# Slots of 256 rows run between the units of attention, with two experts' weights fetched ahead

## The chip, the cores and the metric

The kernel runs on one core of one Trainium2 chip. The metric is the device time of one execution in microseconds; beside it stands one profiled execution, whose trace gives every row shown here. TensorE is called PE (its weight loads PEld), VectorE DVE, ScalarE ACT, GpSimd POOL and SyncE SP.

## What is computed

Block-sorted attention feeds a layer of eight experts, of which each row uses one.

```python
# attention: B, H, S, D = 4, 8, 768, 64; 8 blocks of 96 rows
P = sort_net;  5 times: P = softmax over the last axis, then divided by its sum over the axis before
k_sorted, v_sorted = P applied to the blocks of k and v
attn = softmax(q_block @ k_sorted_block.T / sqrt(D));  x = attn @ v_sorted_block   # x: 3072 x 512
# experts: E, F = 8, 1024
logits = x @ w_gate + modality_bias[modality_id]
e_idx = argmax(logits);  gate_w = softmax(logits)[e_idx]
out[rows of e] = gate_w * (relu(x @ w1[e]) @ w2[e])
```

The inputs drawn for the reference send 1513 of the 3072 rows to expert 0 and 1559 to expert 3; no other expert gets one.

## The kernel before

The order of all instructions on each engine is that of the code (a manual schedule). Three parts follow each other.

Preparation and sort: POOL issues the loads of k, v and q of the first two batches (g = 0). DVE runs the five Sinkhorn steps and puts pieces of `spread_k` between them, which copy k into a zero-padded layout; POOL copies the other half. `make_bd` builds block-diagonal matrices, and the sort multiplies k and v with them, 8 matmuls (k) or 4 (v) into one PSUM bank, with two such banks; each bank is evacuated by `sort_k` or `sort_v` on DVE or ACT.

Attention: 32 units of half the blocks of one head for two batches. A unit has `prep_q` (a spread on DVE, six transposes, a copy), `scores`, `expo` on ACT and `av` with its normalization on DVE. The 28 sort jobs of the other two batches (g = 1) are put into units 2 to 15, two a unit. The gate's transposes and matmuls (`gate_T`, `gate_L`) trail by one octet of units. After each octet m, `choose` finds the expert of each of its 768 rows and `place` scatters the rows to a DRAM scratch sorted by expert, with eight indirect DMAs on POOL. `load_w` is called for experts 0 to 3 behind the first scatter, for all eight after attention and for all eight once more; a flag per expert makes each DMA conditional.

Experts: 25 slots of 128 rows after attention (`run`, lines of `mX`, `mL1`, `mH`, `mL2`). A slot loads its rows with SP, transposes them (line 593), multiplies with w1 (line 599, 8 matmuls of 512 columns, the rows being the stationary side), applies relu, transposes the result (line 626), multiplies with w2 (line 599, 8 matmuls of 512) and scatters the scaled rows to the output. Which expert a slot has stands in a table; PE loads the offset into a register (line 607) and adds a constant to it for each matmul. That addition is an instruction of PE's sequencer of its own (FUSED_REGOPS in the trace, ISA in the order). Slots 0 to 10 need only the first three octets; the last octet's scatter, table and padding (`pad_fill`) run between them.

Of the kernel before, what the change touches and what calls it, by code (L numbers as in the profile page):

```python
# [17 lines left out]
def kernel(  # L18
# [21 lines left out]
    NT = N // 128  # L40
# [3 lines left out]
    CAP = N + 128  # L44
    S1, SU, SMAX = 11, 25, 31
    S2 = SMAX - S1
# [3 lines left out]

    xs_dram = nc.dram_tensor("xs_scratch", [E * CAP + 128, GW // 2], I32, kind="Internal").ap()
# [22 lines left out]
    g_off = k_off + 2 * BLK * D
    xTg = [w_all[:, g_off + z * 768:g_off + (z + 1) * 768].rearrange("p (t r) -> p t r", t=8) for z in range(2)]

    v_sb = [singles.tile([128, 128, VW], BF16, tag=f"v_sb{g}", name=f"v_sb{g}") for g in range(2)]
    v_sbf = [t.rearrange("p x d -> p (x d)") for t in v_sb]
    k_raw = v_sbf[1][:, 0:BLK * D]
    attnT = [singles.tile([96, 8 * BLK + 32], BF16, tag=f"attnT{z}", name=f"attnT{z}") for z in range(2)]  # L80
    xb = [singles.tile([BLK, 8, GW], BF16, tag=f"xb{z}", name=f"xb{z}") for z in range(2)]
    ubuf = singles.tile([128, 8 * 768 + 2 * 1536], BF16, tag="ubuf")

    def qT_buf(g, h):
        base = ubuf if g == 0 else w_all
        x0 = h * 768 + (0 if g == 0 else k_off)
        return base[:, x0:x0 + 768]

    def qil_buf(g, hq):
        if g == 0:  # L90
            return v_sbf[1][:, BLK * D:BLK * D + 1536]
        x0 = k_off + 8 * 768 + (hq % 2) * 1536
        return w_all[:, x0:x0 + 1536]

    qin_bufs = [ubuf[:, 8 * 768 + z * 1536:8 * 768 + (z + 1) * 1536] for z in range(2)]

    ident = singles.tile([128, 128], BF16)
    P_t = singles.tile([BH, NB, NB], FP32)
    nc.sync.dma_start(out=P_t, in_=sort_net.rearrange("b h i j -> (b h) i j"))
    k_src = k.rearrange("b h (n c) d -> (b h n) (c d)", n=NB)  # L100
    v_src = v.rearrange("b h (n c) d -> (b h n) (c d)", n=NB)

    def load_k(g):
        for kc in range(KCH):
            cs = slice(kc * KCW * D, (kc + 1) * KCW * D)
            nc.gpsimd.dma_start(out=k_raw[:, cs], in_=k_src[g * 128:(g + 1) * 128, cs])

    def spread_k(kc, par):
        rows = slice(par * 64, (par + 1) * 64)
        cs = slice(kc * KCW * D, (kc + 1) * KCW * D)  # L110
        eng = nc.gpsimd if par else nc.vector
        eng.tensor_copy(k_il[rows, kc * KCW:(kc + 1) * KCW, par],
                        k_raw[rows, cs].rearrange("p (c d) -> p c d", d=D))

    def load_v(g):
        nc.gpsimd.dma_start(out=v_in, in_=v_src[g * 128:(g + 1) * 128])

    def load_q(g, hq):
        t = qin_bufs[hq % 2].rearrange("p (r h f) -> p r h f", r=2, h=2)
        for par in range(2):  # L120
            nc.gpsimd.dma_start(out=t[:, par], in_=q[2 * g + par, 2 * hq:2 * hq + 2]
                                .rearrange("h (p t) d -> p h (t d)", t=6))
# [26 lines left out]
    bias0 = singles.tile([BLK, E], FP32)  # L149
    nc.sync.dma_start(out=bias0, in_=moe_modality_bias[0:1].broadcast_to([BLK, E]))  # L150
    biasd = singles.tile([BLK, E], FP32)
    nc.sync.dma_start(out=biasd, in_=moe_modality_bias[1:2].broadcast_to([BLK, E]))
    wg_sb = singles.tile([128, 4, E], BF16)

# [9 lines left out]
                   ap=[ident.ap[0], [1, NB], [NB, 16]])  # L164
    for it in range(5):
# [4 lines left out]
        if it == 0:  # L170
            nc.vector.tensor_reduce(jmask, id3s, AX.X, ALU.add)
        elif it == 1:
            nc.vector.tensor_reduce(bmask, id3, AX.X, ALU.add)
            for g in range(2):
                nc.vector.tensor_copy(sel[g], ident[0:BH, g * 16:(g + 1) * 16].broadcast_to([BH, 16, NB]))
        else:
            spread_k(it - 2, 0)
# [9 lines left out]
    bd_v, bd_k = [], []  # L187

    def make_bd(g):
# [9 lines left out]
        bv = singles.tile([128, 16, NB], BF16, tag=f"bdv{g}", name=f"bdv{g}")  # L199
        rb = bass.AP(tensor=rr.tensor, offset=rr.offset, ap=[rr.ap[0], [0, 16], rr.ap[1]])  # L200
        nc.vector.tensor_tensor(bv, bmask.broadcast_to([128, 16, NB]), rb, ALU.mult)
        bk = singles.tile([128, 8, NB], BF16, tag=f"bdk{g}", name=f"bdk{g}")
        nc.vector.tensor_tensor(bk, bv[:, 0:8], bv[:, 8:16], ALU.add)
        bd_v.append(bv.rearrange("p a b -> p (a b)"))
        bd_k.append(bk.rearrange("p a b -> p (a b)"))

    make_bd(0)
    v_cols = v_flat.rearrange("p (c d) -> p d c", d=D)

    def sort_k(g, ch, act):  # L210
        acc = mipsum.tile([128, 8, 64], FP32, tag="mi", name=f"ka{g}_{ch}")
        for z in range(8):
            nc.tensor.matmul(acc[:, z], k_il[:, ch * 8 + z].rearrange("p r d -> p (r d)"), bd_k[g],  # L213
                             start=True, stop=True)
        dst = kTb[g].rearrange("p (x c) -> p x c", c=BLK)[:, :, ch * 8:(ch + 1) * 8]
        (nc.scalar.copy if act else nc.vector.tensor_copy)(dst, acc.rearrange("p z x -> p x z"))  # L216

    def sort_v(g, ch, act):
        acc = mipsum.tile([128, 4, 128], FP32, tag="mi", name=f"va{g}_{ch}")
        for z in range(4):  # L220
            nc.tensor.matmul(acc[:, z], v_cols[:, ch * 4 + z], bd_v[g], start=True, stop=True)  # L221
        dst = v_sb[g][0:BLK, :, ch * 4:(ch + 1) * 4]
        (nc.scalar.copy if act else nc.vector.tensor_copy)(dst, acc[0:BLK].rearrange("p z x -> p x z"))  # L223

    sort_jobs = [[(sort_k, g, ch) for ch in range(12)] + [(sort_v, g, ch) for ch in range(16)]
                 for g in range(2)]
    for n, (f, g, ch) in enumerate(sort_jobs[0]):
        f(g, ch, n % 2)
        if n == 11:
            load_k(1)  # L230
            make_bd(1)
    load_v(1)

    from concourse.masks import make_upper_triangular
    maskUT = singles.tile([128, 128], BF16)
    make_upper_triangular(nc, maskUT, val=1.0, diag=False)
    ones_bf = singles.tile([128, 128], BF16)
    nc.gpsimd.memset(ones_bf, 1.0)
    ones8 = singles.tile([128, E], FP32)
    nc.gpsimd.memset(ones8, 1.0)  # L240
    nc.gpsimd.dma_start(out=wg_sb, in_=moe_w_gate.rearrange("(c p) e -> p c e", p=128))
    ebase = singles.tile([BLK, E, E], BF16)
    nc.gpsimd.memset(ebase, 0.0)
    for e in range(1, E):
        nc.gpsimd.memset(ebase[0:1, :, e:e + 1], float(CAP * e))
    tiew = singles.tile([BLK, E], FP32)
    for e in range(E):
        nc.gpsimd.memset(tiew[:, e:e + 1], float(E - e))
    pI = singles.tile([128, 1], I32)
    nc.gpsimd.iota(pI, pattern=[[0, 1]], base=0, channel_multiplier=1)  # L250
    pF = singles.tile([128, 1], FP32)
    nc.gpsimd.tensor_copy(pF, pI)
    sI = singles.tile([128, SMAX], I32)
# [530 lines left out]
```

## Time and profile before

| | us |
|---|---|
| median of 3 runs (lowest to highest) | 308.87 (305.28 to 310.0) |
| the profiled execution | 309.65 |
| its span, first to last instruction | 307.5 |
| busy: PE, DVE, POOL, ACT | 208.3, 150.0, 113.5, 98.3 |

[...] Instructions of a sequencer (register additions, waits, issues) count as no busy time of their engine.

### The profile page before, as it was taken

How to read it: one execution, taken by the hardware profiler on the slowest of the kernel's cores; microseconds unless marked ns; L12 is line 12 of the kernel's file. 1: busy time of each engine (PE TensorE's matmuls, PEld its weight loads, DVE VectorE, ACT ScalarE, POOL GpSimd, SP SyncE). 2: the span in 40 equal slices, each digit the busy share in tenths (PEclk: the TensorE clock that was granted, in tenths of full speed). 3: DMA queues.
4: the chain of work that ended last, by engine and by line, in shares of the span. 5: the costliest groups of instructions: out<-in, count | busy, mean ns of one | idle time of the engine just before them, and what ended most of it. 6: DMA issues, size and time to landing. Idle time of an engine off the chain costs nothing. (4 is left out here: it accounts for less than half of the span.)

```text
span 307.5 us, 5922 instructions
## 1 busy us (share of the span) xinstructions
PE 208.3 (68%) x1929; PEld 140.3 (46%) x1929; DVE 150.0 (49%) x442; ACT 98.3 (32%) x163; POOL 113.5 (37%) x237
## 2 busy tenths in 40 slices
PE   0007634389998850289770699689949999999930
PEld 0006533277886750277550355345524555555510
DVE  7985537956575560276980255543312323333300
ACT  2003421144756510054420033223422344434420
POOL 8970045504038503074471017812041322333330
PEclk9999999995555555555555599979986999999995
DMA  6998239403402799811120302424153232331110
GB/s 100 224 190 161 47 48 202 61 0 49 59 15 77 115 207 209 133 54 54 29 75 21 103 2 88 130 94 137 55 163 95 71 99 86 106 104 70 50 63 2
DMA packets 21072, 28.05 MB, mean 91 GB/s; under 512 B 5935, under 2 KB 16431, under 8 KB 20784
## 3 DMA queue, kind: packets, MB, share of 16 engines
q0 software_dynamic: 12704, 23.11, 34.7%
q1 hardware_dynamic: 8336, 4.52, 6.1%
q8 instruction: 19, 0.31, 0.4%
q14 instruction: 13, 0.11, 0.1%
HBM read 106.11 MB, written 10.91 MB: 381 GB/s over the span
## 5 line engine op out<-in xcount | busy, mean ns | idle before, releaser
L599 PEld LDWEIGHTS <-ubuf 128*128 128x128 bf16 x400 | 39.1, 101 | 43.2 <-issue 7.9
L599 PE MATMUL hp<-w_all,ubuf 128*128 x200 | 50.0, 395 | 3.3 <-issue 2.4
L645 POOL DMA_INDIRECT out_dram<-v_sb,ix x25 | 24.8, 990 | 70.3 <-ACT ubuf L627 42.2
L599 PE MATMUL yp<-w_all,ubuf 128*128 x200 | 49.8, 394 | 0.4 <-DVE ubuf L627 0.4
L414 POOL DMA_INDIRECT xs_scratch<-xb,dest x32 | 30.2, 943 | 41.5 <-issue 20.4
L616 DVE TENSOR_SCALAR ubuf<-hp 128x512 bf16<-128x512 f32 x25 | 17.3, 692 | 46.0 <-PE hp L599 44.8
L618 ACT ACTIVATE ubuf<-hp 128x512 bf16<-128x512 f32 x25 | 14.9, 597 | 66.5 <-DVE ubuf L616 60.5
L314 ACT ACTIVATE attnT<-sc 96x768 bf16<-96x768 f32 x32 | 25.2, 808 | 17.4 <-PE sc L308 17.4
L329 DVE TENSOR_TENSOR xb<-op,rs 96x256 bf16<-96x256 f32 x64 | 26.9, 420 | 2.2
L637 ACT ACTIVATE v_sb<-yp,v_sb 128x512 f32<-128x512 f32 x25 | 17.2, 687 | 22.3 <-PE yp L599 22.3
L627 DVE COPY ubuf<-ht 128x512 bf16<-128x512 bf16 x25 | 10.6, 423 | 25.5 <-PE ht L626 25.4
L325 PE MATMUL op<-v_sb,attnT 96*128 96x65 bf16 x256 | 20.5, 243 | 0.1
L213 PEld LDWEIGHTS <-w_all 128*128 128x128 bf16 x192 | 11.1, 126 | 19.6 <-issue 19.1
L221 PE MATMUL va<-bdv,w_all 128*128 128x128 bf16 x128 | 17.1, 307 | 4.1 <-DVE v_sb L223 2.1
L593 PE MATMUL mx<-ident,v_sb 128*128 128x128 bf16 x100 | 10.6, 234 | 13.7 <-DMA v_sb<-xs_scratch 13.7
L294 PE MATMUL tq<-ident,w_all 128*128 128x128 bf16 x48 | 6.6, 308 | 18.7 <-DVE w_all L128 18.7
L223 ACT CAST v_sb<-va 96x512 bf16<-96x512 f32 x24 | 13.6, 583 | 16.6 <-PE va L221 15.5
L626 PE MATMUL ht<-ident,ubuf 128*128 128x128 bf16 x200 | 16.7, 226 | 2.6 <-DVE ubuf L594 2.4
L626 PEld LDWEIGHTS <-ubuf 128*128 128x128 bf16 x200 | 14.1, 101 | 9.0 <-issue 3.6
L328 DVE RECIPROCAL rs<-op 96x4 f32<-96x4 f32 x64 | 11.0, 172 | 13.9 <-PE op L325 13.7
L216 ACT CAST w_all<-ka 128x512 bf16<-128x512 f32 x18 | 10.2, 586 | 22.9 <-PE ka L213 22.8
L325 PEld LDWEIGHTS <-attnT 96*128 96x128 bf16 x256 | 17.2, 133 | 0.6 <-DVE xb L329 0.6
(170 smaller groups left out, 308.7 us busy)
## 6 DMA issues: line engine op xcount, KB each, us to landing
w_all<-in_moe_w_dram POOLq DMA_DIRECT2D x40, 1024.0 KB
v_sb<-xs_scratch SPq DMA_DIRECT2D x25, 129.0 KB, 2.0
v_sb<-in_k_dram POOLq DMA_DIRECT2D x6, 512.0 KB
w_all<-in_v_dram POOLq DMA_DIRECT2D x2, 1536.0 KB
ubuf<-in_q_dram POOLq DMA_DIRECT2D x16, 192.0 KB
xs_scratch<-v_sb SPq DMA_DIRECT2D x9, 129.0 KB, 2.2
xs_scratch<-xb,dest POOLq DMA_INDIRECT x32
out_dram<-v_sb,ix POOLq DMA_INDIRECT x25
```

Source lines behind the costliest of these rows:

```text
L221: nc.tensor.matmul(acc[:, z], v_cols[:, ch * 4 + z], bd_v[g], start=True, stop=True)
L223: (nc.scalar.copy if act else nc.vector.tensor_copy)(dst, acc[0:BLK].rearrange("p z x -> p x z"))
L314: nc.scalar.activation(attnT[u % 2][:, 0:8 * BLK].rearrange("p (r f) -> p r f", r=2), sc_tiles.pop(u)[0:BLK, :, 0:4 * BLK], ACT.Exp, scale ...
L325: nc.tensor.matmul(op[:, j], attnT[u % 2][:, c0:c0 + 128], v_sb[g][0:BLK, par * 64 + h * 8 + i, 0:D + 1], start=True, stop=True)
L329: nc.vector.tensor_tensor(xt[:, par * 4:(par + 1) * 4, h * D:(h + 1) * D], op[0:BLK, :, 0:D], rs.broadcast_to([BLK, 4, D]), ALU.mult)
L414: ins = nc.gpsimd.indirect_dma_start(out=xs_dram, out_offset=bass.IndirectOffsetOnAxis(ap=dest[:, t:t + 1], axis=0), in_=xt.bitcast(I32)[: ...
L599: ins = nc.tensor.matmul(*a, **kw).ins
L616: nc.vector.tensor_scalar(hd, hp[:, half], 0.0, None, ALU.max)
L618: nc.scalar.activation(hd, hp[:, half], ACT.Relu)
L626: nc.tensor.transpose(tp[:, c], h_b[s % 2][:, fc * 128:(fc + 1) * 128], ident)
L637: nc.scalar.activation(y, yp, ACT.Copy, scale=xt.bitcast(FP32)[:, Dm // 2 + 1:Dm // 2 + 2])
L645: ins = nc.gpsimd.indirect_dma_start(out=out, out_offset=bass.IndirectOffsetOnAxis(ap=ix, axis=0), in_=y, in_offset=None, bounds_check=N - ...
```

## The change

The program is rewritten around five things.

1. Nothing of k is spread any more. `sort_k` multiplies k as it was loaded, once for each of the two batches, into the two halves of the partitions: 16 matmuls of 64 columns where 8 were. PSUM is divided anew: four banks `mi` for everything, one pair `sc`, one pair `op`. The first sort uses all of them.
2. The two experts with the largest biases of the two modalities are taken as "home" experts and renumbered 0 and 1 (`home_map`). Their weights alone get a buffer, `w01`. The first is fetched after the first sort, the second in unit 9 behind the first scatter, with all of q of the other batches behind it.
3. Slots have 256 rows and belong to one octet each: 2, 3, 3 and 5 slots, 13 in all. A table of 18 small operations on DVE is made after each octet.
4. `mL1` multiplies with the weights as the stationary side and the rows as the moving one (256 columns), so that its result is transposed already; `mH` is gone. A slot has 8 transposes, 32 matmuls of 256 columns and 16 of 512.
5. A slot is cut into seven pieces, and the pieces are put between the parts of the units: three a unit in units 14 to 18, two a unit in units 22 to 31, the other 57 after attention. Rows that those slots leave over go through a general loop at the end, which the drawn inputs do not enter: 1513 rows make 6 slots and 1559 make 7.

The core of the diff:

```diff
-    S1, SU, SMAX = 11, 25, 31
+    PR = 256
+    SLOTS = [(0, 2), (2, 3), (5, 3), (8, 5)]
+    NS = 13
...
-    scpsum = ctx.enter_context(tc.psum_pool(name="scpsum", bufs=2))
-    opsum = ctx.enter_context(tc.psum_pool(name="opsum", bufs=2))
-    mipsum = ctx.enter_context(tc.psum_pool(name="mipsum", bufs=2))
+    scpsum = ctx.enter_context(tc.psum_pool(name="scpsum", bufs=1))
+    opsum = ctx.enter_context(tc.psum_pool(name="opsum", bufs=1))
+    mipsum = ctx.enter_context(tc.psum_pool(name="mipsum", bufs=4))
...
+        for z in range(n):
+            for par in range(2):
+                nc.tensor.matmul(acc[par * 64:(par + 1) * 64, z], k_raw[:, (c0 + z) * D:(c0 + z + 1) * D],
+                                 bd[g][:, par * 64:(par + 1) * 64], start=True, stop=True)
...
+    def load_w(z, tab=None, n=None, parts=(0, 1)):
+        tb, n = (etab, z) if tab is None else (tab, n)
+        er = nc.values_load(tb[0:1, n:n + 1], engines=(PoolEng,), min_val=0, max_val=E - 1)
+        v1, v2 = w_views(z)
+        if 0 in parts:
+            nc.gpsimd.dma_start(out=v1, in_=moe_w1[bass.ds(er, 1)].rearrange("o (c p) f -> p (o c) f", p=128))
...
-                w_mm(s, hp[:, half], xT_b[s % 3][:, c],
-                     w_all[:, bass.ds(ev + (c * F + half * 512), 512)], start=(c == 0), stop=(c == 3))
+    def mL1(s, j):
+        ev = evs[s]
+        hp = mipsum.tile([128, 2, PR], FP32, tag="mi", name=f"hp{s}_{j}")
+        for f in range(2):
             for c in range(4):
+                nc.tensor.matmul(hp[:, f], w_at(ev, c * F + (2 * j + f) * 128, 128), xT_b[s % 2][:, c],
+                                 start=(c == 0), stop=(c == 3))
...
+            at2(8 * m + 9, choose, m)
+            at2(8 * m + 9, place, m)
+            at1(8 * m + 10, table_x, m)
+    at2(9, load_w, 1)
+    at2(9, load_q, 1, 0)
+    at2(9, load_q, 1, 1)
...
+    pieces = []
+    for s in range(NS):
+        if s == 0:
+            pieces.append([(mE, (0,)), (mX, (0,))])
+        for j in range(4):
+            pieces.append([(mL1, (s, j))])
+        if s + 1 < NS:
+            pieces.append([(mE, (s + 1,)), (mX, (s + 1,))])
+        pieces.append([(mL2, (s, 0))])
+        pieces.append([(mL2, (s, 1))])
...
+        if u < 14:
+            return 0, 0
+        if u < 19:
+            return 2, 1
+        if u < 22:
+            return 0, 0
+        return 1, 1
...
+        p1, p2 = pace(u)
+        scores(u)
         expo(u)
+        for f, a in A1.get(u, []):
+            f(*a)
+        run_pieces(p1)
+        if u >= 1:
+            av(u - 1)
         prep_q(u + 2)
+        for f, a in A2.get(u, []):
+            f(*a)
+        run_pieces(p2)
```

How the rows stand on the engines shows in three places. On PE, the first matmuls of a slot before, where `ubuf` is the transposed rows and `w_all` the weights:

```order
L607 TENSOR_LOAD tab_462
L607 ISA x2
L599 LDWEIGHTS ubuf
L599 ISA
L599 MATMUL hp_2397<-w_all,ubuf 128x512
L599 LDWEIGHTS ubuf
L599 ISA
L599 MATMUL hp_2397<-w_all,ubuf 128x512
```

and of the change, where `w_72` is the buffer `w01` and `qT_76` holds the transposed rows:

```order
L572 ISA
L572 LDWEIGHTS w_72
L572 ISA
L572 MATMUL hp_0_1547<-qT_76,w_72 128x256
L572 ISA
L572 LDWEIGHTS w_72
L572 ISA
L572 MATMUL hp_0_1547<-qT_76,w_72 128x256
```

The register addition stood once per matmul of 512 columns; it stands twice per matmul of 256, since the weight load now has the address that is known only at run time. On POOL, in unit 9 of the change, the last of eight scatters (line 439), then the second weight (lines 529 to 534) and q (line 116):

```order
L439 DMA xs_scratch<-xb_85,dest_1206 26880x258
L529 TENSOR_LOAD etab
L529 ISA x2
L532 ISA
L532 DMA w_72<-in_moe_w_dram 128x4x1024
L534 ISA
L534 DMA w_72<-in_moe_w_dram 128x8x512
L116 DMA q_in_80<-in_q_dram 128x4x384 x4
```

Before, q of the same batches stood behind four conditional weights, of which two moved bytes; now it stands behind one. On PE at the start of unit 18 of the change, the last scores (line 340), the count for the table (line 460), and the transposes of the rows of slot 2 (line 553):

```order
L340 MATMUL sc_1887<-qT_77,kT_75 128x96
L460 LDWEIGHTS ones_bf
L460 MATMUL cp_1897<-ohs_129,ones_bf 128x8
L560 TENSOR_LOAD tabE_241
L560 ISA x2
L553 LDWEIGHTS xt_91
L553 MATMUL mx_1958<-ident,xt_91 128x128
```

The transposes of slot 2 stand there in PE's order ahead of the second layer of slot 1 and of the unit's own `av`; the scatter that fills the rows of slot 2 was issued in unit 17.

## Rows read from the trace of the kernel before

**Rows 1.** Stretches of the span: busy time (instructions) of each engine, granted clock, DMA share, GB/s.
```profile
core 0: us, PE busy (x) PEld busy (x) DVE busy (x) ACT busy (x) POOL busy (x), PEclk, DMA share, GB/s
0.00:22.90 22.90, 0.23 (x2) 0.23 (x3) 19.91 (x44) 2.56 (x6) 20.23 (x24) 1.00 1.02 171
22.90:42.90 20.00, 14.35 (x161) 12.46 (x160) 10.49 (x18) 8.19 (x14) 0.34 (x1) 1.00 0.43 82
42.90:64.40 21.50, 8.88 (x110) 7.55 (x110) 15.44 (x33) 3.18 (x5) 12.05 (x35) 1.00 0.68 111
64.40:111.70 47.30, 42.09 (x562) 36.27 (x561) 29.84 (x103) 25.51 (x43) 16.97 (x30) 0.54 0.39 69
111.70:128.20 16.50, 0.45 (x9) 0.23 (x8) 2.35 (x11) 0.95 (x2) 2.55 (x5) 0.50 1.21 204
128.20:161.20 33.00, 27.95 (x365) 22.58 (x365) 26.23 (x110) 12.99 (x18) 17.97 (x33) 0.50 0.17 48
161.20:170.40 9.20, 0.00 (x0) 0.00 (x0) 0.68 (x3) 0.00 (x0) 1.06 (x13) 0.50 0.12 37
170.40:229.90 59.50, 49.15 (x311) 26.16 (x311) 24.30 (x81) 18.29 (x31) 20.62 (x53) 0.90 0.29 95
229.90:296.20 66.30, 65.18 (x416) 34.87 (x416) 20.79 (x43) 26.58 (x45) 20.68 (x44) 0.96 0.26 86
296.20:307.50 11.30, 0.00 (x0) 0.00 (x0) 0.00 (x0) 0.00 (x0) 0.99 (x1) 0.68 0.05 16
```

**Rows 2.** Timeline of DVE in the Sinkhorn steps: start, duration, what.
```profile
8.24 4.42 DVE L112 COPY w_all<-v_sb 64x2048 bf16<-64x2048 bf16 x1
```

**Rows 3.** Timeline of PE in the sort: start, duration, line, matmuls, idle time before.
```profile
24.24 1.01 PE L213 MATMUL ka<-bdk,w_all 128*128 128x64 bf16 x16 [0.35 <-DVE w_all L216]
...
33.08 1.01 PE L221 MATMUL va<-bdv,w_all 128*128 128x128 bf16 x8 [0.67 <-ACT v_sb L223]
```

**Rows 4.** Groups by line: evacuations of the sort; busy us, mean ns of one.
```profile
L223 ACT CAST v_sb<-va 96x512 bf16<-96x512 f32 x24 | 13.6, 583 | 16.6 <-PE va L221 15.5 <-issue 1.1
...
L223 DVE CAST v_sb<-va 96x512 bf16<-96x512 f32 x8 | 5.5, 686 | 4.8 <-PE va L221 4.8
```

**Rows 5.** Timeline of POOL: loads of a weight, then two scatters of a run of eight.
```profile
100.84 0.81 POOL L451 DMA_DIRECT2D w_all<-in_moe_w_dram  x1
101.65 0.94 POOL L452 DMA_DIRECT2D w_all<-in_moe_w_dram  x1
...
131.44 0.98 POOL L414 DMA_INDIRECT xs_scratch<-xb,dest  x1 [13.10 <-issue]
...
132.91 0.94 POOL L414 DMA_INDIRECT xs_scratch<-xb,dest  x1 [0.28 <-POOL xb L413]
```

**Rows 6.** Line 599 in one slot, 243.3 to 245.3: duration min/median/max, first and last start.
```profile
L599 PEldq FUSED_REGOPS  x16: 42/46/46, 243.3 to 245.2; - x16
...
L599 PE MATMUL hp<-w_all,ubuf x8: 376/378/380, 243.4 to 244.9; 128*128 x8
```

**Rows 7.** Line 607, the load of a slot's offset by PE's sequencer: as in rows 6.
```profile
L607 PEldq TENSOR_LOAD <-tab x25: 298/302/572, 170.4 to 288.3; - x25
L607 PEldq FUSED_REGOPS  x25: 151/151/165, 171.0 to 288.8; - x25
```

**Rows 8.** Chain that ended last, in time: start, duration; slot 0, then a late slot.
```profile
171.87 3.59 PE hp L599 x8
...
255.99 1.79 PE hp L599 x8
257.78 0.22 PE mx L593 x4
258.00 1.73 PE yp L599 x8
259.73 0.45 PE ht L626 x8
```

**Rows 9.** DMA issues: count, KB each, us from issue to landing.
```profile
v_sb<-xs_scratch SPq DMA_DIRECT2D x25, 129.0 KB, 2.0
```

More of the change, by code (lines that the diff above doesn't have):

```diff
@@ L84, in qT_buf @@
[L84 to L95, printed above, removed]
+    xTg = [singles.tile([128, 8, BLK], BF16, tag=f"xTg{z}", name=f"xTg{z}") for z in range(2)]
@@ L108, in spread_k @@
[L108 to L122, printed above, removed]
@@ L169 @@
         nc.scalar.activation(P_t, P_t, ACT.Exp)
[L170 to L177, printed above, removed]
+        for f in gap[it]:
+            f()
         nc.vector.tensor_reduce(red, P_t, AX.X, ALU.add)
@@ L204, in make_bd @@
-        bd_v.append(bv.rearrange("p a b -> p (a b)"))
-        bd_k.append(bk.rearrange("p a b -> p (a b)"))
+        bd.append(bv.rearrange("p a b -> p (a b)"))
     make_bd(0)
[L208 to L215, printed above, removed]
-        (nc.scalar.copy if act else nc.vector.tensor_copy)(dst, acc.rearrange("p z x -> p x z"))
@@ L227 @@
[L227 to L253, printed above, removed]
@@ new lines, in sort_v, with jobs @@
+    def sort_v(g, d0, kind, act):
+        n = 4 if kind == "mi" else 8
+        acc = psum_t(kind, f"va{g}_{d0}").rearrange("p (z x) -> p z x", x=128)
+        for z in range(n):
+            nc.tensor.matmul(acc[:, z], v_cols[:, d0 + z], bd[g], start=True, stop=True)
+        dst = v_sb[g][0:BLK, :, d0:d0 + n]
+        (nc.scalar.copy if act else nc.vector.tensor_copy)(dst, acc[0:BLK].rearrange("p z x -> p x z"))
+    def jobs(g, kinds):
+        res, c0, d0 = [], 0, 0
+        for kd in kinds:
+            if c0 < BLK:
+                res.append((sort_k, g, c0, kd))
+                c0 += 8 if kd == "mi" else 16
+            else:
+                res.append((sort_v, g, d0, kd))
+                d0 += 4 if kd == "mi" else 8
+        assert c0 == BLK and d0 == D
+        return res
@@ L563 @@
[L563 to L578 removed]
+        n_s = SLOTS[m][1]
@@ new lines, with in_xs_group, zero_block @@
+    zsrc = zpad.bitcast(I32)
+    zsrc2 = bass.AP(tensor=zsrc.tensor, offset=zsrc.offset, ap=[zsrc.ap[0], [0, 2], zsrc.ap[1]])
+    def in_xs_group(ins, keep=()):
+        kw = {"keep": list(keep)} if keep else {}
+        tc.declare_no_dep(ins, group="xs", reason="rows are disjoint or ordered by hand", **kw)
+        tc.add_to_no_dep_group("xs", ins)
+    def zero_block():
+        ins = nc.sync.dma_start(out=xs_dram[ZR:ZR + PR].rearrange("(p t) w -> p t w", t=2), in_=zsrc2)
+        in_xs_group(ins.ins)
+        pads.append(ins.ins)
@@ L590, in mX @@
     def mX(s):
-        tp = mipsum.tile([128, 4, 128], BF16, tag="mi", name=f"mx{s}")
-        for c in range(4):
-            nc.tensor.transpose(tp[:, c], xt_b[s % XB][:, c * 128:(c + 1) * 128], ident)
-        nc.vector.tensor_copy(xT_b[s % 3], tp)
-    p1_mm = []
-    def w_mm(s, *a, **kw):
-        ins = nc.tensor.matmul(*a, **kw).ins
-        if s < S1:
-            for d in w_dma[3]:
-                tc.declare_no_dep(ins, d, reason="experts of this slot were loaded before")
-            p1_mm.append(ins)
@@ L649, in mL2, with bal @@
         tc.add_to_no_dep_group("out", ins.ins)
-    todo = {}
-    def at(u, f, *a):
-        todo.setdefault(u, []).append((f, a))
+    def bal(lst):
+        load, res = [0.0, 0.6], []
+        for f, g, x0, kd in lst:
+            c = (0.59, 0.69) if kd == "mi" else (1.02, 1.22)
+            z = 0 if load[0] + c[0] <= load[1] + c[1] else 1
+            load[z] += c[z]
+            res.append((f, g, x0, kd, z == 0))
+        return res
+    from concourse.masks import make_upper_triangular
+    maskUT = singles.tile([128, 128], BF16)
@@ new lines @@
+    m_, s_, o_ = "mi", "sc", "op"
+    g0 = bal(jobs(0, [s_, o_, m_, m_, m_, m_, s_, o_,
+                      m_, m_, s_, m_, m_, o_, m_, m_, s_, m_, m_, o_]))
+    for n, (f, g, x0, kd, act) in enumerate(g0):
+        f(g, x0, kd, act)
+        if n == 16:
+            prep_q(0)
+    load_k(1, 0)
+    load_k(1, 1)
+    make_upper_triangular(nc, maskUT, val=1.0, diag=False)
+    nc.gpsimd.iota(pI, pattern=[[0, 1]], base=0, channel_multiplier=1)
+    nc.gpsimd.iota(idI, pattern=[[BLK, NTL]], base=0, channel_multiplier=0)
@@ new lines, with x_try, table_x, at1 @@
+    st = {"tab": -1, "x": 0, "done": 0, "pos": 0}
+    def x_try():
+        while st["x"] < NS:
+            s = st["x"]
+            i, n = slot_tab(s)
+            if i > st["tab"] or s - 3 >= st["done"]:
+                return
+            x_load(s, (scat[i] + pads if n == 0 else ()))
+            st["x"] += 1
+    def table_x(m):
+        table(m)
+        if m == 3:
+            pad_fill(0)
+            pad_fill(1)
+        st["tab"] = m
+        x_try()
+    A1, A2 = {}, {}
+    def at1(u, f, *a):
+        A1.setdefault(u, []).append((f, a))
@@ new lines, in run_pieces, with pace @@
+    def run_pieces(n, upto=NS):
+        for _ in range(n):
+            if st["done"] >= upto or st["pos"] >= len(pieces):
+                return
+            for f, a in pieces[st["pos"]]:
+                f(*a)
+                if f is mL2 and a[1] == 1:
+                    st["done"] = a[0] + 1
+                    x_try()
+            st["pos"] += 1
+    def pace(u):
+        if u < 14:
[5 more added lines that the diff above has]
+        return 1, 1
@@ L702 @@
-        av(u)
-    nc.gpsimd.memset(zrow, 0.0)
-    nc.sync.dma_start(out=xs_dram[E * CAP:E * CAP + 128], in_=zrow.bitcast(I32))
-    for e in range(EH, E):
-        load_w(2, e)
-    for s in range(XB):
-        x_load(s, scat[0] + scat[1] + scat[2] if s == 0 else ())
-    def load3():
-        make_flags(3)
-        for e in range(E):
-            load_w(3, e)
-        for d in w_dma[3]:
-            for i_ in p1_mm:
-                tc.declare_no_dep(d, i_, reason="experts of those slots were loaded before")
@@ L741 @@
-    run(list(range(SU)))
+        run_pieces(p2)
+    run_pieces(1)
+    av(31)
+    run_pieces(2)
+    gate_T(3, 3)
+    run_pieces(1)
+    gate_L(3, 3)
+    choose(3)
+    run_pieces(1)
+    place(3)
+    run_pieces(2)
+    table_x(3)
+    run_pieces(1000)
     order.close()
-    n2 = nc.values_load(nT2[0:1, 0:1], min_val=0, max_val=S2)
+    n2 = nc.values_load(nrem[0:1, 0:1], min_val=0, max_val=NREST)
     rest = ExitStack()
-    for s in range(SU, SMAX):
-        rest.enter_context(tc.If(n2 > s - S1))
-        x_load(s)
+    rest.enter_context(tc.If(n2 > 0))
@@ new lines, with row_b @@
+    for e in range(2, E):
+        pad_fill(e, own=False)
+    dm2 = singles.tile([1, NREST, E], FP32)
+    tR2 = singles.tile([1, NREST], I32)
+    tE2 = singles.tile([1, NREST], I32)
+    ci = small.tile([1, E], FP32, tag="r_ci", name="r_ci")
+    ce = small.tile([1, E], FP32, tag="r_ce", name="r_ce")
+    ga = small.tile([1, E], FP32, tag="r_ga", name="r_ga")
+    i2 = small.tile([1, NREST, E], FP32, tag="r_i2", name="r_i2")
+    rv = small.tile([1, NREST], FP32, tag="r_rv", name="r_rv")
+    def row_b(ap):
+        return bass.AP(tensor=ap.tensor, offset=ap.offset, ap=[ap.ap[0], [0, NREST], ap.ap[1]])
@@ L749 @@
         mX(s)
-        mL1(s)
-        mH(s)
-        mL2(s)
+        for j in range(4):
+            mL1(s, j)
+        for t in range(2):
+            mL2(s, t)
     rest.close()
```

647 lines of the change are left out of this document (311 added, 336 removed).

## The prediction

> **What bounds the kernel now.** I read the stretches first [rows 1]. The reader is to see three kinds. Up to 64.4 us DVE and POOL prepare (DVE 19.91 of 22.90) and PE is fed slowly. From 64.4 to 161.2 attention runs; PE is busy 42.09 of 47.30 and 27.95 of 33.00, but at the lower clock (0.50 to 0.54), and between them lies a hole of 16.5 us in which the DMA engines are the busy part (share 1.21, 204 GB/s): q waits behind two experts' weights. From 161.2 on comes a wait of 9.2, then the experts (59.5 + 66.3), in which PE is full at the upper clock, and a tail of 11.3. Then I read the chain that ended last: a late slot is hp 1.79, mx 0.22, yp 1.73, ht 0.45, together 4.2 us for 128 rows with nothing between [rows 8]. So attention is PE at half clock with idle DVE and ACT, and the experts are PE alone at full clock. Overlapping them can win only what PE leaves idle now: the hole, the wait, the slack in attention, and the clock.
>
> The record of the clock begins at 1.00, but 8 va matmuls of 128 columns in the sort take 1.01/8 = 126 ns apiece [rows 3], where 4 mx of 128 columns late in the run take 0.22/4 = 55 [rows 8]; 512 columns at the start of the experts take 3.59/8 = 0.45 us, and late 1.73/8 = 0.216 [rows 8]. So I price the sort at the lower level.
>
> **The change, part by part.** Start: of DVE's chain up to 22.9 the three spreads go (the first took 4.42 [rows 2]), with the drag of POOL's copies; some 16 small operations and as many memsets of 0.1 to 0.2 us come. Net about -6: the sort begins at 17 (range 15 to 20).
>
> First sort, now 20.0 [rows 1]: evacuation alone is the lower bound: 28 banks shared by an ACT at 583 ns and a DVE at 686 ns [rows 4], 28/(1/0.583 + 1/0.686) = 8.8. PE alone is the upper one: 192 matmuls for k at 1.01/16 = 63 ns and 64 for v at 126 [rows 3] are 12.1 + 8.1 = 20.2. I take 15, between the two: k's matmuls have doubled, but the 63 and 126 hold the drain of each run's last matmul. It ends at 32, with the first scores at 32.5. That is 10 us gained over 42.9.
>
> Units 0 to 13: units 4 to 19 took 47.3 [rows 1], 2.96 each, with 28 sort jobs in them, so 14 units are 41. Added: 12 k jobs x 8 more matmuls x 63 ns = 6, less a drain each, 5; a table of 18 small operations on DVE at about 0.2, 4. Unit 14 begins at 82.5.
>
> The first wait. `place` in unit 9 falls at about 67. A scatter takes 132.91 - 131.44 = 1.47 a piece [rows 5], eight take 11.8, to 79. Only then does POOL issue the second weight (0.81 + 0.94 [rows 5]) and q. The order shows that the first piece of layer one waits for this weight, as its address is known only at run time, and unit 14's `prep_q` for q. 2.1 + 0.8 MB at 173 to 204 GB/s (the hole's rate [rows 1] is the upper one) take 14 to 17: 96. PE stands about 9.5 us where it stood 16.5 before.
>
> Units 14 to 17: PE in attention is 27.95/12 = 2.3 a unit [rows 1]; four units are 8, `choose` and `place` 2. Pieces: 7 of layer one at 1.84 (below), one set of transposes 0.9, two of layer two at 3.4 at the lower clock (8 x 0.43): 20.6. So 127.
>
> The second wait. In unit 18 the transposes of slot 2 stand in PE's order ahead of everything else, and the scatter of octet 1 was issued only in unit 17, at about 124.5. Plus 11.8, plus 2 for its landing, plus 0.4 + 2.0 for loading the rows [rows 9]: 141. PE stands 12 us. Then two pieces of layer two and `av`: 150. Units 19 to 21 have no pieces: 157.
>
> Units 22 to 31: attention 23; 12 pieces of layer one 22, 3 of transposes 2.7, 5 of layer two 17: 65 at the lower clock. At the upper one 41. I take 54 (the mix raises the clock at times): 211. The gate and `place` of the last octet add 4, the last piece of slot 4 2: 217.
>
> **The price of a slot** is the term that decides. PE's matmuls of a slot of 256 rows at the upper clock are 32 x 0.108 + 16 x 0.216 + 8 x 0.056 = 7.4 (halves and eighths of rows 8), against 2 x 4.2 = 8.4 now. But each dynamic address costs PE's sequencer. In one slot 16 register additions run from 243.3 to 245.2 while the matmuls they serve end later: 1.9/15 = 127 ns apiece, of which the addition itself is 46 [rows 6]. Before, that hid under matmuls of 216 ns. Layer one now has two additions for a matmul of 108 ns. Bounds: if only the body adds, 127 + 46 = 173 ns; if all of it doubles, 254. I take 230, near the upper end, because four transposes' loads and matmuls stood among those 16 without raising the period, so the period belongs mostly to the addition. A piece is 8 x 0.23 = 1.84, a slot 32 x 0.230 + 16 x 0.127 + about 0.75 for loading the offset (302 + 151 + 18 ns and gaps [rows 6, 7]) = 10.2. The trace has no two additions in one matmul, so neither bound is shown.
>
> Eight slots stay behind attention: 8 x 10.2 = 82, plus 4 for stretches at the lower clock: 303. The tail is as before, 11.3 [rows 1]: span 314. The profiled run lay 2.2 outside its span and 0.8 above the median: **316 us**.
>
> What is hidden: ACT and DVE get two relus each a slot (0.7 apiece) and fewer copies, under 3 us in 10; POOL's output scatters 2 x 1.5 a slot. Without PE's slowness they would still not bind. The last octet's scatter (16 us with landing and load) lies under three slots (30).
>
> **Rivals.** *Cheap addresses* (0.25): the second addition costs little more than its body, 186 ns or less a matmul, and the clock stays up. A slot is then 7.4 (PE) to 32 x 0.186 + 2.03 + 0.75 = 8.7; 8 x 1.5 to 2.8 less, and about 5 less in the units: 289 to 299, 293 in the middle. For it: the body is 46 of 127 ns. Against: four transposes more left the period as it was. [...]
>
> *Waits that vanish* (0.10): DMA is quicker than I price it, or the units before are slower, so that weights, q and rows of slot 2 are there; layer one at my price. 316 less most of 9.5 + 12: 298. Against: the scatter's 11.8 us stand on POOL ahead of both.
>
> *The clock falls in the slots* (0.18): layer one leaves PE idle between matmuls, the clock goes to 0.50 as in attention, where PE was busy 42.09 of 47.30 and stayed there [rows 1]. Then a slot is 32 x 0.23 + 16 x 0.43 + 1 = 15, or half of that loss: 8 x 2.4 to 4.8 more: 335 to 354. For it, the mixed stretches; against, layer two is dense.
>
> *No change in sum* is the forecast's own low edge: 10 us gained at the start, 7 in the hole and the 9.2 wait, against 12 at the second wait and a dearer slot.
>
> **How the numbers follow.** The forecast (sequencer bound, two waits) has 0.47 and a range of its own of 303 to 330. About 2% is what a measurement of this kernel tells from no change: 303 to 315. Of the forecast's mass 0.27 lies above 315, 0.17 within and 0.03 below. Faster: 0.25 + 0.08 + 0.03 = 0.36; slower: 0.18 + 0.27 = 0.45; same 0.17 + 0.02 = 0.19. The range of 286 to 340 takes in the first two rivals and the near half of the third.
>
> **What would show it.** In the trace after: layer one's matmuls about 230 ns apart at clock 1.00 with PE idle "issue" between them; register additions twice per matmul; a hole on PE in unit 14 ended by the weight's or q's DMA, and one in unit 18 ended by a load from the scratch; slots after attention 10 us apart. Matmuls 108 ns apart would make the price of a slot wrong, holes under 5 us the timeline, and a late clock of 0.5 the third rival right.

## The result, and the profile after

The changed kernel is faster. It took 288.24 us (median of 4 runs, 286.73 to 289.6) where the kernel before took 309.44 beside it: a ratio of 0.9385, 95% interval 0.925 to 0.952. In a later set of runs the two took 291.17 and 310.29: 0.945 (0.934 to 0.957). Every ratio leaves out executions that lie over 1.5% above the fastest of their kernel, so it differs a little from the quotient of the medians. The profiled execution took 289.21, its span 287.5.

The stretches of the changed kernel, cut where its stages change. Columns as in [rows 1]: start and end, length, then busy time (instructions) of PE, PE's weight loads, DVE, ACT and POOL, then the granted clock, the DMA share and GB/s.

```profile
core 0: us, PE busy (x) PEld busy (x) DVE busy (x) ACT busy (x) POOL busy (x), PEclk, DMA share, GB/s
0.00:14.60 14.60, 0.24 (x4) 0.26 (x6) 11.20 (x71) 2.56 (x6) 6.34 (x15) 1.00 0.87 158
14.60:28.90 14.30, 12.59 (x268) 12.13 (x267) 8.63 (x12) 7.80 (x11) 0.26 (x1) 0.92 1.32 175
28.90:77.70 48.80, 34.83 (x615) 29.79 (x614) 34.25 (x110) 23.15 (x38) 14.92 (x29) 0.64 0.67 132
77.70:94.70 17.00, 3.85 (x34) 2.42 (x34) 2.61 (x6) 1.65 (x3) 2.77 (x5) 0.50 1.18 211
94.70:119.40 24.70, 20.76 (x206) 13.26 (x206) 11.73 (x33) 6.58 (x11) 2.59 (x4) 0.91 0.21 46
119.40:134.70 15.30, 0.38 (x10) 0.15 (x4) 2.72 (x18) 1.15 (x2) 8.94 (x16) 0.50 0.28 71
134.70:150.00 15.30, 12.01 (x136) 7.66 (x136) 7.93 (x19) 4.37 (x6) 2.37 (x4) 0.83 0.21 68
150.00:189.80 39.80, 36.34 (x405) 23.05 (x405) 20.68 (x66) 15.34 (x23) 13.66 (x24) 0.92 0.20 62
189.80:272.40 82.60, 77.95 (x491) 42.45 (x489) 23.81 (x66) 22.05 (x35) 28.71 (x49) 1.00 0.26 82
272.40:287.50 15.10, 0.00 (x0) 0.00 (x0) 0.00 (x0) 0.01 (x1) 1.22 (x3) 0.61 0.10 34
```

Two holes in PE's work stand out (77.7 to 94.7 and 119.4 to 134.7), in the two places that were forecast. PE's timeline shows what ended them. Columns: start, duration, line, what, and in brackets the idle time before with its releaser.

```profile
84.96 1.04 PE L553 MATMUL mx<-ident,xt 128*128 128x128 bf16 x8 [6.85 <-DMA xt<-xs_scratch]
...
94.69 0.82 PE L324 MATMUL tq<-ident,q_il 128*128 128x128 bf16 x6 [5.32 <-DVE q_il L123]
```

The first hole holds two waits: for the rows of slot 0 and for q (through DVE's spread of it). The second, before the transposes of slot 2, is in the table of PE's waits:

```profile
PE mx L553 <- DMA xt<-xs_scratch: 21.8, 2, 14.9
```

That is two waits, 21.8 us together, the longest 14.9: the shorter one is the wait for the rows of slot 0 above. The chain that ended last shows the late slots:

```profile
220.49 3.45 PE yp L584 x16
223.95 5.15 PE hp L572 x32
229.10 0.42 issue
229.52 0.62 PE mx L553 x8
230.14 3.45 PE yp L584 x16
```

A slot of 256 rows takes 230.14 - 220.49 = 9.65 us here, and 9.8 in those after it, where two slots of 128 took 8.4 before [rows 8].

**Where the 20.0 us of span went** (307.5 to 287.5). To compare attention, I take 34/7 slots of 9.8 us, 47.6, as the cost of the 34 pieces that run up to 189.8 us, since that is what they cost behind attention. (By the code 35 of the 91 pieces stand between the units and 56 behind them, not 57; the cut lies ahead of the last of the 35.) PE's idle time counts as the wait in each hole.

| part | before [rows 1] | after | difference |
|---|---|---|---|
| to the first scores | 42.9 | 28.9 | -14.0 |
| attention without pieces and holes | 118.3 - 16.05 = 102.25 | 160.9 - 47.6 - 28.1 = 85.2 | -17.05 |
| holes (before with the 9.2 wait) | 25.25 | 13.15 + 14.9 = 28.05 | +2.8 |
| experts | 125.8 | 47.6 + 82.6 = 130.2 | +4.4 |
| tail | 11.3 | 15.1 | +3.8 |

So experts, holes and tail all became dearer. The gain is the start and attention. Attention's part holds an assumed price for the pieces and cannot be read off one trace; the experiments are mostly about it.

### The profile page after: what moved, and what is told of

It is laid out like the page before. It is cut to its first block, busy times and chain, and to the rows that moved or that the text cites. A ratio compares the mean times of both kernels' runs of the same rounds, so it can differ in the third digit from the quotient of the medians.

```text
span 287.5 us, 6499 instructions
## 1 busy us (share of the span) xinstructions
PE 198.9 (69%) x2150; PEld 131.2 (46%) x2150; DVE 123.6 (43%) x397; ACT 84.7 (29%) x133; POOL 81.8 (28%) x147
## 4 chain that ended last, share of the span: by engine, by line
PE 40%; DVE 4%; issue 2%; DMA 2%; ACT 1%; POOL 1%; POOLq 0%; DVEq 0%; SPq 0%; ACTq 0%
PE hp L572 19%; PE yp L584 14%; PE mx L553 2%; PE gt L370 1%; PE op L358 1%; PE sc L340 1%; DVE xb L362 1%; DMA xt<-xs_scratch 1%; DMA xs_scratch<-xb,dest 1%; PE lg L376 1%; POOL out_dram L591 1%; DVE qT L576 0%; PE tq L324 0%; ACT attnT L346 0%; ACT y L588 0%
## 5 line engine op out<-in xcount | busy, mean ns | idle before, releaser
L572 PE MATMUL hp<-qT,w 128*128 128x256 bf16 x416 | 74.6, 283 | 1.5 <-DVE qT L554 1.0
L591 POOL DMA_INDIRECT out_dram<-y,ix x26 | 25.8, 993 | 107.2 <-ACT y L588 80.3
L572 PEld LDWEIGHTS <-w 128*128 x416 | 40.4, 100 | 30.7 <-issue 4.3
L584 PE MATMUL yp<-w,qT 128*128 x208 | 49.3, 389 | 0.0
L576 DVE TENSOR_SCALAR qT<-hp 128x512 bf16<-128x512 f32 x26 | 17.9, 690 | 50.2 <-PE hp L572 50.2
L588 ACT ACTIVATE y<-yp,xt 128x512 f32<-128x512 f32 x26 | 17.9, 687 | 57.3 <-PE yp L584 52.2
L578 ACT ACTIVATE qT<-hp 128x512 bf16<-128x512 f32 x26 | 15.5, 596 | 64.6 <-PE hp L572 64.6
L584 PEld LDWEIGHTS <-qT 128*128 128x128 bf16 x208 | 19.9, 100 | 21.8 <-issue 1.7
L553 PE MATMUL mx<-ident,xt 128*128 128x128 bf16 x104 | 8.9, 234 | 25.2 <-DMA xt<-xs_scratch 21.8
L362 DVE TENSOR_TENSOR xb<-op,rs 96x512 bf16<-96x512 f32 x32 | 22.0, 686 | 1.3 <-DVE rs L361 0.2
L324 PE MATMUL tq<-ident,q_il 128*128 128x128 bf16 x96 | 10.2, 257 | 17.2 <-DVE q_il L123 17.2
L358 PEld LDWEIGHTS <-attnT 96*128 96x128 bf16 x256 | 13.4, 110 | 4.2 <-DVE xb L362 1.7
L294 PE MATMUL va<-bd,kvb 128*128 128x128 bf16 x128 | 14.2, 285 | 0.1
```

The lines of the kernel that those rows point to most:

```text
L324: nc.tensor.transpose(tp[:, t], src[:, t], ident)
L358: nc.tensor.matmul(ov[:, par, j], attnT[u % 2][:, c0:c0 + 128], v_sb[g][0:BLK, par * 64 + h * 8 + i, 0:D + 1], start=True, stop=True)
L362: nc.vector.tensor_tensor(xt[:, :, h * D:(h + 1) * D].rearrange("p (r j) d -> p r j d", r=2), ov[0:BLK, :, :, 0:D], rs.broadcast_to([BLK, ...
L553: nc.tensor.transpose(tp[:, c, t * 128:(t + 1) * 128], xt_b[s % 3][:, t, c * 128:(c + 1) * 128], ident)
L572: nc.tensor.matmul(hp[:, f], w_at(ev, c * F + (2 * j + f) * 128, 128), xT_b[s % 2][:, c], start=(c == 0), stop=(c == 3))
L576: nc.vector.tensor_scalar(hd, hp, 0.0, None, ALU.max)
```

## The experiments

Absolute times are compared between kernels measured beside a kernel before of about 310 us; one set ran on a chip where it took 316.87, and there ratios are used.

**Is it the interleaving?** All pieces run after attention:

```
     def pace(u):
-        if u < 14:
-            return 0, 0
-        if u < 19:
-            return 2, 1
-        if u < 22:
-            return 0, 0
-        return 1, 1
+        return 0, 0
```

> The changed kernel with no piece between the units of attention: all 91 pieces run after unit 31; everything else stays. Theory (what PE gains by the interleaving is small and the second wait takes it back): in the changed kernel the stretch from 94.7 to 189.8 us is 95 us for 18 units and 34 pieces, of which 15 are the wait. Without pieces the 18 units take about 2.3 us each at the lower clock (41 us, as the units late in the kernel before), the first wait still ends at 94.7 by q's arrival, attention ends at 137, and 13 slots of 9.8 us (127) and a tail of 15 follow: about 282 us, between 276 and 288. Rival (the interleaving is what made the change faster, by filling PE and by holding the clock up): 298 us or more. The granted clock of units 22 to 31 tells whether the pieces held it up: 0.92 with them, 0.5 expected without.

298.67 us, ratio 0.966 (0.960 to 0.971), beside 310.13 before: 7 to 10 more than with pieces (288.24 and 291.17). My theory fell, and the rival of 298 or more came true. The theory's error is in the units: I had priced 18 of them at 2.3 us, and they took from 94.5 to 150.0, 3.08 each. PE stands 18.0 us in that stretch, 15.5 of them for DVE, which spreads q, chooses the experts and makes the tables in between. Units 22 to 31 in this kernel, with the scores that begin unit 22 and the transposes that begin slot 0 behind unit 31:

```profile
122.10:150.00 27.90, 18.39 (x253) 15.32 (x252) 16.66 (x60) 9.93 (x13) 9.00 (x16) 0.50 0.14 39
```

```profile
122.14 0.50 PE L340 MATMUL sc<-qT,kT 64*128 64x96 bf16 x8
...
150.03 1.03 PE L553 MATMUL mx<-ident,xt 128*128 128x128 bf16 x8
```

They take 27.9 us at clock 0.50; in the changed kernel they take 39.8 with pieces between them, at 0.92. The pieces alone, 20 of them, are 20/7 x 9.8 = 28.0, so with them the units cost 11.8: 16 us less than alone.

**Is that the clock?** To the kernel without pieces I added eight matmuls of 128x512 on fixed operands in each of the units 22 to 31:

```
         if u >= 1:
             av(u - 1)
+        if u >= 22:
+            fl = mipsum.tile([128, 512], FP32, tag="mi", name=f"fl{u}")
+            for _ in range(8):
+                nc.tensor.matmul(fl, ident, w01[:, 0:512], start=True, stop=True)
```

> The changed kernel without pieces between the units, and with eight matmuls of 128x512 on fixed operands, whose result nobody reads, added to each of the units 22 to 31. At the upper clock eight such take 1.73 us on PE, at the lower about 3.5. Theory (what the pieces give attention is above all the clock: without them it was 0.50 there and PE busy 16.0 of 24.9 us): the filler raises the granted clock of units 22 to 31 to 0.8 or more, the ten units' own work shrinks, and the time grows over the kernel without pieces by 3 to 10 us where the filler alone is 17 at the upper clock. Rival (the clock does not answer to it, or it fills idle time only): clock stays at 0.50, 35 us of filler less at most 9 of idle time, 24 to 35 us more.

The whole kernel took 319.47 us, ratio 1.012 (1.007 to 1.017), on the chip where the kernel before took 316.87; the kernel without pieces did not run there, so I compare the stretch. Two units in it (23 and 24), then all ten:

```profile
131.53:136.91 5.38, 5.38 (x66) 3.15 (x66) 2.46 (x6) 1.61 (x2) 0.00 (x0) 1.00 0.00 0
127.20:164.40 37.20, 31.07 (x332) 17.12 (x331) 16.68 (x59) 9.80 (x13) 9.01 (x16) 0.90 0.08 22
```

The clock answers: 0.90, and 1.00 in the middle. There two units with two fillers (3.45 us by the price of layer two, eight of 512 columns) take 5.38, so a unit's own work is 0.97 us; without filler two units take 4.52 at 0.50. The scores of units 29, 30 and 31 stand on PE's timeline of the kernel without pieces, those of 29 and 31 here:

```profile
142.51 0.50 PE L340 MATMUL sc<-qT,kT 64*128 64x96 bf16 x8 [0.41 <-ACT attnT L346]
...
147.03 0.50 PE L340 MATMUL sc<-qT,kT 64*128 64x96 bf16 x8 [0.41 <-ACT attnT L346]
```

The ten units grew by 37.2 - 27.9 = 9.3 us for 17.3 of filler, inside the theory's 3 to 10 and far from the rival's 24 to 35. (The 24.9 us of the expectation begin in unit 23, so they miss a part of the ten.) Two of the ten fillers still ran at the lower level (3.5 us each, where the other eight took 1.89), and waits for DVE stayed. So of the 16 us that pieces save in units 22 to 31, the clock is one part and filled idle time the other. PE's 18.39 us of busy time would be about 9.2 at the upper level (an estimate, half of it, from the fillers' 1.89 us for 3.5), which is 9 us; and PE idles 9.5 of 27.9 us without pieces and 3.5 of 39.8 with them, which is 6.

**What are the two holes worth?** First the second one, alone. The pieces are reordered so that the transposes of slot 2 come behind both parts of layer two of slot 1, in unit 22:

```
-        if s + 1 < NS:
-            pieces.append([(mE, (s + 1,)), (mX, (s + 1,))])
+        nx = [[(mE, (s + 1,)), (mX, (s + 1,))]] if s + 1 < NS else []
+        if s != 1:
+            pieces.extend(nx)
         pieces.append([(mL2, (s, 0))])
         pieces.append([(mL2, (s, 1))])
+        if s == 1:
+            pieces.extend(nx)
...
-            return 2, 1
+            return 2, (0 if u == 18 else 1)
```

> The changed kernel with the transposes of slot 2 (whose rows the scatter of octet 1 writes) moved behind both pieces of layer two of slot 1, so that they are the first piece of unit 22 and no longer stand in unit 18. Theory (PE stands 15 us in unit 18 only since these transposes come first in its order, and units 18 to 21 with the two pieces are work that covers the scatter): the hole at 119 to 135 us closes but for 0 to 3 us, and the time falls by 10 to 14, to about 276. Rival (the scatter and the load end later, or units 18 to 21 wait for something else that the hole hid, such as the q of later heads): the hole moves to unit 22 and the time stays within 4 us of 288.

276.04 us, ratio 0.890 (0.884 to 0.896). The wait before those transposes, in unit 22 now:

```profile
135.26 1.03 PE L553 MATMUL mx<-ident,xt 128*128 128x128 bf16 x8 [0.85 <-DMA xt<-xs_scratch]
```

The rows come when they came before (135.3 against 134.7); four units and two pieces of layer two stand ahead of them now. A hole of 15 us hung on the place of one piece in PE's order.

Then the first hole, alone:

```
     load_w(0)
+    load_w(1)
+    load_q(1, 0)
+    load_q(1, 1)
     prep_q(1)
...
-    at2(9, load_w, 1)
-    at2(9, load_q, 1, 0)
-    at2(9, load_q, 1, 1)
```

> The changed kernel with the second home expert's weights and the second half of q issued on POOL right behind the first expert's weights (into buffers that nothing else uses), not behind the scatter of octet 0. Theory (the first wait, 77.7 to 94.7, is the arrival of q, which waited behind eight scatters and beside 2 MB of weights): q is there by 78, PE waits only for the rows of slot 0, which then come at 80 to 82 instead of 85 since no weight is moving beside them; the wait shrinks by 8 to 12 us, and the time to 276 to 280. Rival (the transfers only move: they now lie beside the loads of k and v of the second half and make the sort of that half late): units 5 to 13 grow by about as much, and the time stays within 4 us of 288.

283.84 us, ratio 0.914 (0.907 to 0.922): 4 to 7 less than the changed kernel, half of what I expected. The wait for q is gone, that for the rows of slot 0 is not. POOL's timeline shows why, in the scatter of octet 0, and so does the median time from a scatter's issue to its landing there, 11.4 us:

```profile
70.19 0.93 POOL L439 DMA_INDIRECT xs_scratch<-xb,dest  x1 [1.31 <-DMA w<-in_moe_w_dram]
71.12 0.20 POOL L438 COPY xb<-idI 96x1 int32<-96x1 int32 x1
72.14 0.94 POOL L439 DMA_INDIRECT xs_scratch<-xb,dest  x1 [0.82 <-DMA q_in<-in_q_dram]
```

```profile
xs_scratch<-xb,dest POOLq DMA_INDIRECT x8, 11.4
```

And PE's, in unit 14:

```profile
83.35 1.03 PE L553 MATMUL mx<-ident,xt 128*128 128x128 bf16 x8 [5.01 <-DMA xt<-xs_scratch]
```

Weights and q are still arriving there (in this profile the DMA moves 198 to 218 GB/s from 60 to 75 us), and POOL's scatters wait for them; over the whole changed kernel the median landing of a scatter is 2.5 us. The rows came at 83.35 instead of 84.96.

Both edits together:

> Both edits that helped alone, together: the transposes of slot 2 behind layer two of slot 1, and the second expert's weights and second half of q fetched early. If the two waits are separate, their gains add (12.2 and 4.4): 271 to 272. If closing one only lets the other begin earlier (the scatter of octet 1, or DMA, is late next), 274 to 277.

286.70 us, ratio 0.908 (0.904 to 0.912), on the chip where the kernel before took 316.87. There it is not below the 0.890 that late rows alone gave elsewhere, so this run can't tell whether the gains add; the next ones can. On the same chip, the pieces also begin later:

```
-        if u < 14:
+        if u < 16:
             return 0, 0
-        if u < 19:
+        if u < 21:
             return 2, 1
-        if u < 22:
-            return 0, 0
         return 1, 1
```

> As the run with both edits, and the pieces begin in unit 16 and not in unit 14: three a unit in units 16 to 20 and two a unit from 21 to 31. In the run with early weights PE stood 5.0 us in unit 14 for the rows of slot 0, behind which the scores of unit 15 were queued. Theory (units 14 and 15 without pieces cover the arrival of these rows): the wait goes, 265 to 269 us. Rival (units 14 and 15 then run at the lower clock, and what they gain is lost since the pieces come later): 270 to 273.

Ratio 0.884 (0.881 to 0.888); 280.83 us there, 5.9 less than with both edits alone. Beside the changed kernel, on a chip with the kernel before at 310.29:

> The changed kernel itself, on the same chip as the three runs beside it, since the chip of the runs filler, late_early, best and no_rest took 316.87 us for the kernel before (310 on the others) and showed register additions of up to 0.7 us on PE's sequencer during the scatters. If this chip is like the first, 286 to 290 and no addition over 0.06 us; if it is like the second, a ratio of 0.95 to 0.965 to the kernel before, which would also explain that the run without the general loop had 0.951.

> The kernel with late rows of slot 2, early weights and q, and pieces from unit 16, beside the changed kernel on one chip. Both waits (13 and 15 us) are gone in its earlier trace, of which 2 us are spent again in a later unit 14: 16 to 22 us less than the changed kernel beside it. Rival (the gain lies in the chip's noise, as the ratio of 0.884 is only just below the 0.890 of the run with late rows alone): 12 to 15 less.

The changed kernel took 291.17 us, 1 more than the 286 to 290 expected of a chip like the first, with no register addition over 0.051 us. The other took 265.52, ratio 0.864 (0.854 to 0.874): **25.7 less than the changed kernel, and by the ratio about 42 less than the kernel before.** More than I expected. Its stretches around the former holes, up to the end of attention:

```profile
78.00:86.00 8.00, 6.71 (x90) 5.87 (x90) 4.53 (x11) 3.41 (x6) 0.02 (x1) 0.57 0.31 78
86.00:130.00 44.00, 35.49 (x339) 21.97 (x336) 21.20 (x67) 12.36 (x19) 14.04 (x24) 0.88 0.20 61
130.00:150.00 20.00, 16.25 (x191) 10.37 (x187) 12.24 (x47) 7.92 (x12) 5.76 (x10) 0.91 0.11 38
150.00:185.00 35.00, 34.02 (x313) 19.62 (x313) 18.60 (x64) 10.83 (x17) 15.43 (x27) 1.00 0.30 95
```

Units 14 and 15 run mostly at the lower clock (0.57 in the first stretch) while the rows of slot 0 land; from there PE has no wait longer than 2.9 us.

With the holes out of the way, what is the interleaving worth? The kernel with early weights and no pieces in attention:

> No pieces between the units, and the second expert's weights and q fetched early: all layers of all slots after attention, with no wait for q. Set against the run before it, it prices the interleaving alone, without either wait. Theory (pieces hold the clock up and fill PE, 20 pieces in units 22 to 31 saved about 12 us and the 15 in units 16 to 20 about 7): 15 to 22 us more than the run with both edits, that is within 4 us of the changed kernel. Rival (the interleaving only pays for its own waits): within 8 us of the run with both edits.

284.15 us, ratio 0.923 (0.912 to 0.933): 18.6 more than the run beside it. So interleaving buys 18.6 us where nothing waits for it. The changed kernel gets 7 to 10 from it (298.67 without pieces). The second hole, which the pieces made, takes the rest: with it closed and the first one kept (late rows, 276.04) the pieces buy 22.6; with it kept, and 5 us of the first, and q early (283.84 against these 284.15) they buy nothing.

**What sets a slot?** Layer one's addresses are fixed, so that every slot, the second expert's too, multiplies with the first home expert's weights in layer one:

```
     def mL1(s, j):
-        ev = evs[s]
+        ev = None
```

> Layer one's weights at an address that is known when the program is built: every slot takes the first home expert's weights in layer one (so what is computed differs there for the second expert's slots). Layer two keeps its address from the table. Theory (the two register additions of a layer-one matmul, on PE's sequencer, set its pace: 208 ns a matmul where PE needs 108): a slot after attention falls from 9.8 us to 7.9 to 8.1, the eight of them by 14, the five in the units by up to 8 more, and the time to 266 to 274. Rival (PE or its weight loads pace layer one, additions run beside them): slots stay at 9.8, time within 3 us of 288.

272.62 us, ratio 0.877 (0.869 to 0.884). In the changed kernel's slot, by line, and then in this one's:

```profile
L572 PEldq FUSED_REGOPS  x46: 46/46/46, 223.9 to 228.7; - x46
```

```profile
223.43 3.19 PE yp L584 x14
226.61 3.49 PE hp L572 x32
230.82 3.19 PE yp L584 x14
```

Additions start every 4.8/45 = 107 ns, two for a matmul: 213 ns. With fixed addresses 32 matmuls take 3.49 us, 109 ns each, and a slot 7.40. It is the sequencer, 2.3 to 2.4 us a slot: 1.7 in layer one itself, the rest in the gap and the transposes ahead of layer two.

**The tail.** The general loop at the end, which the drawn inputs don't enter, is left out (its count and all behind it):

> The changed kernel without the general loop at the end, which the drawn inputs do not enter. Theory (the tail of 15.1 us behind the last layer-two result, where the kernel before has 11.3, holds some 4 us for loading the loop's count on every engine, the branch past it, and code): the tail shrinks to 10 to 12 and the time by 3 to 5, to about 284. Rival (the tail is the landing of the last scatter and the closing steps, which stay): tail 14 to 15, time within 1.5 us of 288.

> The kernel without the general loop, beside the changed kernel on one chip. The earlier trace has 9.8 us behind the last layer-two result where the changed kernel has 15.1. Theory (the general loop's count and branch make 4 to 5 us of the tail): 4 to 6 us less than the changed kernel beside it. Rival (the tail was shorter for another reason of that chip): less than 2 us.

The first run took 301.96 us, a ratio of 0.951 on the chip of 316.87, which says nothing without the changed kernel there. Beside the changed kernel it took 284.66 against 291.17: 6.5 less, a little above the 4 to 6 expected. The last result of layer two, in the changed kernel and then in this one:

```profile
271.72 0.69 ACT L588 ACTIVATE y<-yp,xt 128x512 f32<-128x512 f32 x1 [1.04 <-PE yp L584]
```

```profile
270.42 0.69 ACT L588 ACTIVATE y<-yp,xt 128x512 f32<-128x512 f32 x1 [1.04 <-PE yp L584]
```

The spans end at 287.5 and 280.1: 15.1 and 9.0 us later. The changed kernel of this second set has 14.8 us there. So a loop that never runs costs about 6 us, with its count and its branch at the end. Which of the two it is was not tried.

## Why the prediction was wrong

It forecast 316 us, slower, with 0.45 for slower and 0.36 for faster; it came out 6% faster. That 288 lies inside the range of 286 to 340 is luck: the low end stood there for the rival of cheap addresses, and addresses were not cheap (213 ns a matmul). By the forecast's own steps, in span:

| step | forecast | measured |
|---|---|---|
| first scores | 32.5 | 28.9 |
| unit 14 begins | 82.5 | 77.7 |
| first wait ends | 96 | 94.7 |
| transposes of slot 2 | 141 | 134.7 |
| units 18 to 21 end | 157 | 150.0 |
| units 22 to 31, length | 54 | 39.8 |
| from there to the end of the last slot | 92 | 82.6 |
| tail | 11.3 | 15.1 |

- **Right:** the places of both waits, and what ends the second and about how long it is (12 forecast, 14.9 measured); that the sequencer paces layer one; that one slot of 256 rows costs more than two of 128 did. The first wait was right in part: PE stands 13.15 us where 9.5 were forecast, and 6.85 of them are for the rows of slot 0, which the forecast did not name beside the weight and q.
- **Units 22 to 31 are the step that failed** (14 of the 26.5 us that the span lay under its forecast; 7 more had come before unit 22, 9 came in the slots, and the tail took 4 back). I took 54 as a mix of 41 at the upper clock and 65 at the lower; the terms at the upper clock (11.5 + 22 + 1.4 + 8.7) come to 44, not 41. It was 39.8 at clock 0.92, below both. The error was in reading [rows 1]: PE busy 42.09 of 47.30 at 0.54 looked like dense work that still left the clock low. Busy time at the lower level is stretched (in the kernel before, eight matmuls of 512 columns take 3.59 us where the clock reads 0.50 and 1.79 where it reads 1.00 [rows 8]): the busy share of 89% is near that of the mixed units (36.34 of 39.8, 91%, at 0.92), but the work, share times clock, is 0.48 against 0.84. Attention's ten units alone were even dearer than I had them (27.9, not 23). The pieces added work, and the clock rose: 0.50 without them, 0.92 with them, 0.90 with fillers in their place. The rival of a falling clock had 0.18 and rested on the same reading.
- **The slots** cost 9.8, not 10.2, and needed no 4 us for the lower clock (1.00 throughout). Two additions take 213 ns on the sequencer, not 230, and 18 of a slot's 64 additions ran under layer two (46 fall into the stretch of layer one), so that layer one's 32 matmuls take 5.15 us, not 7.4. The rival of cheap addresses is added up with 186 ns or less a matmul. No run shows that figure: a matmul took 213 ns with its two additions and 109 with none (fixed addresses).
- **The start** was 3.6 us shorter, and 2.4 of that lie ahead of the sort, which began at 14.6 and not at 17: DVE's chain lost more than I took off. The sort itself took 14.3 where I had 15, between two bounds of which the upper was too high. For that one I priced the sort's matmuls of k at 63 ns from [rows 3], the lower level. After:

```profile
14.56 5.33 PE L285 MATMUL ka<-bd,kvb 128*64 128x64 bf16 x192 [0.90 <-DVE bd L240]
```

28 ns each: half as long, the clock at 0.92 over the sort. It looks like the same error again, a price read at one clock and used for a denser stretch; but the stationary side is half as wide here (128*64, before 128*128), so no run shows that the clock alone made the difference.
- **The tail** I called unchanged. The diff shows what was added there, a loop with a count to load, and I took the tail over "as before" without naming a cover.

## What to carry to other kernels

Before pricing a merge of two phases, convert PE's busy time at the lower clock into work: 89% busy at 0.54 is 48% of what PE can do, and filling it can pay twice, in idle time and in clock (here about 6 and 9 us, estimated above). Where a piece of work is interleaved by hand, look at the first instruction of each piece that needs a far result, and put the work that covers the flight ahead of it: here one reordering was worth 12 to 15 us (276.04 against 288.24 and 291.17). Price what stands at the very end, even if it never runs (here about 6 us).

## What the runs showed of the hardware

On one of the chips PE's sequencer stumbled, mostly while POOL scattered the last octet. In the kernel without the general loop these scatters run from 212.5 to 223.2 us and the slow additions lie between 215 and 228; on another chip the same kernel, which scatters the same octet, has no addition of line 572 over 0.051 us in its whole run, so scattering alone does not explain it. Line 572 in that kernel on that chip, and then in nearly the same stretch on another one (durations in ns, min/median/max):

```profile
L572 PEldq FUSED_REGOPS  x40: 3/16/697, 215.8 to 227.9; - x40
```

```profile
L572 PEldq FUSED_REGOPS  x99: 42/46/51, 214.0 to 227.4; - x99
```

The one did 40 additions in 12.1 us and the other 99 in 13.4. All four kernels that ran there show additions of 0.70 to 0.86 us at the longest in that line, and on the other chips none over 0.051; the kernel before was 2% slower there as well, of which no trace was taken. What the sequencer waits for there is open: no run shows it.
